# Relayout transfers that write every sixth row, into four tensors of their own

## The chip, the cores and the metric

The kernel runs on one core of a Trainium2 chip. The metric is device time in microseconds of one execution; lower is better. The kernel before took 726.89 us, the median of three runs (723.93 to 726.97).

## The reference

Three layers run one after the other, on 4 sequences of 768 positions.

```python
# 1. gated linear attention with a complex decay: 8 heads of 48
for t in range(S):
    ar, ai = (a_re_n[:, :, t, :, None], a_im_n[:, :, t, :, None])
    new_re = ar * S_re - ai * S_im
    new_im = ar * S_im + ai * S_re
    kv = np.einsum('bhd,bhe->bhde', k[:, :, t], v[:, :, t])
    S_re, S_im = (new_re + kv, new_im)
    y[:, :, t] = np.einsum('bhd,bhde->bhe', q[:, :, t], S_re)
# 2. feed-forward, 384 -> 1024 -> 384, gated by a convolution of 3 positions
h = np.maximum(x @ w_in, 0.0)
...
x = h * gate @ w_out
# 3. four experts of causal attention (width 64), the best two of each position summed
...
out += mask[..., None] * w[:, :, kk:kk + 1] * ye
```

## The kernel before

The recurrence is computed in chunks of C = 128 positions. A unit is UC = 2 chunks (256 positions); there are 12 units, three for each sequence. For each unit `e_ops` turns the decays into magnitudes and phases (`polar`, `phase`: running sums by matmuls with a triangle, L423, then exponentials and sines), and `rotate` multiplies q and k with them (`c.mul`, the helper at L380). The result of `rotate` lies with 384 rows (head dimension by head) as 3 tiles of 128 partitions. The chunk matmuls need it with 48 real and 48 imaginary rows on 96 partitions and the 8 heads beside each other. `put` does this relayout by DMA, from SBUF to SBUF: for kT and qT, real and imaginary half, one transfer for each of the 3 tiles, so 12 for a unit. A transfer reads 128 partitions and writes 16 rows of 8 heads. All are recorded by the helper at L386, and nearly all are issued on SP's queue; in the profile they are `arena_Z<-arena_F`.

For each chunk `m_ops` then multiplies scores out of kT and qT (L571, masked on VectorE at L573), transposes kT (L583, copied at L585), forms the state (L591, L600) and the output (L609 and L613, copied at L619), which goes to a scratch tensor in HBM. Stage two (`s2_ops`) loads it in half sequences and runs the feed-forward by nine matmuls a block up (L743) and nine down (L781). Stage three (`s3_ops`) projects (L851, L901), scores, takes softmaxes and sums.

No order is written out by hand. Each `S.op` names its engines with a cost in microseconds, the tiles it reads and writes, and a priority made of the numbers in the table `P` (`tu` is the pitch of units, `lag` the start of stage two in units, `u0`, `v0`, ... corrections for single units). `Sched.run` is a list scheduler on a model of the engines: it chooses for each op the time, the engine among those named, and the address, and `emit` writes the instructions in that order. On the chip each engine then runs its own list in order and waits on semaphores. Transfers are modelled as one pipe of 360 GB/s behind the issue, and land 0.9 us after it; a relayout counts 512 bytes for each column.

Tiles lie in arenas: F (float32), R (float32r, for stages two and three) and Z, which is used as float32 by stage one (Z0: kT, qT, v, masked scores, states) and as float32r (Z1) by the later stages once no op of stage one needs it (L148). While stage two's first loads are awaited, TensorE runs idle-filling matmuls on zeros (L627).

The lines of the relayout:

```python
r0 = 48 * half + 16 * i
c.load(lambda r0=r0: dst[r0:r0 + 16, :, x0:x1], lambda i=i: src[:, i, x0:x1], 512 * (x1 - x0), ...
```

Of the kernel before, what the change touches and what calls it, by code (L numbers as in the profile page):

```python
# [9 lines left out]
F32 = mybir.dt.float32  # L10
F32R = mybir.dt.float32r
# [27 lines left out]
P = dict(tu=24.81, lag=2.00, tf=3.56, dn=29.40, pa=28.16, pf=31.70, pp=31.74, ps=19.16, pr=12.98, kn=9.82, pd=-10.31,
         py=-3.49, cw=6.45, cs=6.91, ne=3, sw=16.78, slack=0.33, hold=1.18, wl=0.23, bl=0.07, bc=0.37, hy=7.13,  # L40
         tb=28.68, xp=-22.98, jq=-1.01, jp=3.08, jv=-4.00, ja=-2.33, jf=16.61, jt=5.79, ju=0.10, jw=0.26, na=13, no=3,
         nt=6, ns=4, nx=7, nq=14, th=0.46, fr=0.20, nc=3, sd=1, ck=-587.37, up=61.76, big=0, a0=1, a1=3, u0=-1.81,
         u1=0.00, u2=3.11, u3=0.02, u4=0.75, u5=-0.59, u6=-1.33, u7=0.35, u8=0.63, u9=-4.21, u10=-7.57, u11=2.39,
         v0=-0.17, v1=-0.88, v2=2.18, v3=0.27, v4=1.22, v5=1.18, v6=0.00, v7=-7.38, v8=-7.08, v9=-2.05, v10=0.00,
         v11=-2.62, b0=0.00, b1=-4.24, b2=-0.23, b3=-0.03, b4=-0.60, b5=-0.53, b6=-3.32, b7=-1.31, b8=-2.61, c0=0.92,
         c1=-2.99, c2=1.81, c3=-0.52, pw=0.34, sp=1.00, jg=-8.86, pm=-0.26)
TABS = {"E": "natural_log_exp_and_others", "T": "trig_and_small", "S": "sigmoid_and_others",
        "U": "silu_and_others", "X": "exp_and_others"}
CPY = ("ACT", "DVE", "POOL")
COLS = {"F": 19200, "R": 16420, "Z": 16200}  # L50


class Tl:
# [41 lines left out]
class Sched:  # L95
# [8 lines left out]
        self.newest, self.fifo = {}, False  # L104

    def tile(self, shape, dtype=F32, tag=None, bufs=0, regs=None, trim=0):
        t = Tl(self, shape, dtype, regs or (("R", "Z1") if dtype == F32R else ("F",)), tag, bufs, trim)
        self.tiles.append(t)
        return t

# [34 lines left out]

    def place(self, t, live, z0):
        for reg in t.regs:
            if reg == "Z1" and z0:  # L148
                continue
            k = reg[0]  # L150
            pos = 0
            for a, b, _ in live[k]:
                if a - pos >= t.size:
                    break
                pos = max(pos, b)
            if self.cap[k] - pos >= (t.size if k == "P" else max(t.size, t.n)):
                return reg, pos
        return None

    def run(self):  # L160
# [5 lines left out]
        live = {k: [] for k in self.cap}  # L166
        counts, frees, left, gops = {}, [], {}, {}
        dma, curtab, now, port, narrow = 0.0, None, 0.0, 0.0, 0.0
        z0 = sum(1 for t in self.tiles if t.left and "Z0" in t.regs)
        for o in self.ops:  # L170
            if o.nd == 0:
                for e in o.alts:
# [25 lines left out]
        while done < total:  # L198
# [11 lines left out]
            while frees and frees[0][0] <= now:  # L210
                _, _, t = heapq.heappop(frees)
                live[t.reg[0]].remove((t.off, t.off + t.size, t.tag))
                counts[t.tag] -= 1
                if "Z0" in t.regs:
                    z0 -= 1
            pick = None
            later = inf
# [172 lines left out]
def s1_ops(c):  # L390
# [10 lines left out]
    def e_ops(u):  # L401
# [6 lines left out]
        F, R = S.tile([128, KT, UT], tag="F", bufs=2, regs=zs), S.tile([128, KT, UT + 4], tag="R", bufs=2, regs=zs)  # L408
        w, n = S.tile([128, KT, UT], tag="w", bufs=2, regs=zs), S.tile([128, KT, UT], tag="n", bufs=2, regs=zs)
        q, k = S.tile([128, KT, UT], tag="q", bufs=1, regs=zs), S.tile([128, KT, UT + 4], tag="k", bufs=1, regs=zs)  # L410
        qT = S.tile([96, H, UT], tag="qT", bufs=2, regs=zr)
        kT = S.tile([96, H, UT + 4], tag="kT", bufs=2, regs=zr)
        v = S.tile([128, UC, H, 64], tag="v", bufs=2, regs=zr)
        parts = [(x, x + 1) for x in range(UC)] if u == 0 else [(0, UC)]
        t.update(qT=qT, kT=kT, v=v, last=(len(parts) - 1, None),
# [96 lines left out]
        def rotate(z, a, b):  # L512
# [11 lines left out]
            def put(dst, half, src, ext):  # L524
                x0, x1 = a * C, b * C + (UC if ext else 0)
                for i in range(KT):
                    r0 = 48 * half + 16 * i
                    c.load(lambda r0=r0: dst[r0:r0 + 16, :, x0:x1], lambda i=i: src[:, i, x0:x1], 512 * (x1 - x0),
                           [(dst, (z, r0))], pr + 2, r=ks(src) + ([(src, (9,))] if ext else []), dur=0.65,
                           gp=u < P["sd"])  # L530

# [501 lines left out]
def tile_kernel(ctx: ExitStack, tc: tile.TileContext, q, k, v, a_re, a_im,  # L1033
# [210 lines left out]
```

## Time and profile before

| what | value |
|---|---|
| median of three runs | 726.89 us |
| the profiled execution | 726.38 us |
| its span | 724.6 us |
| mean granted clock of TensorE | 0.952 of full speed |
| busy: TensorE, VectorE, ScalarE, GpSimd | 665.6, 563.1, 486.8, 86.7 us |
| SP's DMA queue | 75.04 MB, 44.3% of 16 DMA engines' span |

The span begins with the first instruction and ends with the last; some 1.8 us of the execution's time lie around it. Stage one and the part of stage two woven into it take the first 395 us, what is left of stage two some 65, and stage three the rest. An engine that is busy need not be the bound: it runs its list in order, and what ends the idle time before an instruction shows what it waited for. [...]

### The profile page before, as it was taken

The page shows a single profiled execution, that of the slowest core. Times are in us where ns is not written, and L with a number is a line of the kernel's source. Part 1 is how long each engine was busy: PE and PEld are TensorE (multiplying, and loading weights), DVE is VectorE, ACT ScalarE, POOL GpSimd, SP SyncE. Part 2 cuts the span into 40 slices and gives each one's busy share as a digit, 9 for nine tenths or more (in the row PEclk, how much of TensorE's full clock was granted, in tenths as well). Part 3 has the DMA queues.
Part 4 walks back from the last instruction along what each step waited for, and adds up shares of the span by engine and source line. Part 5 has one row for each costly group of instructions (what it writes and reads, how often), then busy time and mean ns, then how long its engine had stood idle before and what let it go on. Part 6 is the DMA issues. An engine that isn't in the chain of part 4 may idle for free.

```text
span 724.6 us, 13162 instructions
## 1 busy us (share of the span) xinstructions
PE 665.6 (92%) x4776; PEld 594.4 (82%) x4780; DVE 563.1 (78%) x1157; ACT 486.8 (67%) x1011; POOL 86.7 (12%) x139
## 2 busy tenths in 40 slices
PE   7789879889798898989999999999999999999995
PEld 4468668779798798889989999997787889888774
DVE  6975889799897897887864899978786666866761
ACT  7944984679578797697842676556756755865752
POOL 0621111021210111300100110001002100100101
PEclk9985997999999999999999999999999999999998
DMA  8967794955929938939383233020003000000002
GB/s 298 156 157 155 214 189 77 234 122 127 208 85 176 241 111 178 164 123 130 125 98 99 94 100 89 33 66 34 1 1 99 33 3 32 34 1 1 34 34 71
DMA packets 54603, 76.57 MB, mean 106 GB/s; under 512 B 5104, under 2 KB 45936, under 8 KB 54528
## 3 DMA queue, kind: packets, MB, share of 16 engines
q1 hardware_dynamic: 54240, 75.04, 44.3%
q0 software_dynamic: 288, 0.59, 0.5%
q8 instruction: 39, 0.64, 0.4%
q14 instruction: 36, 0.29, 0.2%
HBM read 42.51 MB, written 14.16 MB: 78 GB/s over the span
## 4 chain that ended last, share of the span: by engine, by line
PE 50%; DVE 9%; DMA 6%; ACT 3%; issue 1%; SPq 1%; POOL 0%; ACTq 0%; DVEq 0%; POOLq 0%
PE banks L781 8%; PE banks L743 6%; PE banks L958 5%; PE banks L901 5%; PE banks L1024 4%; DMA arena_Z<-arena_F 4%; PE banks L851 3%; PE banks L979 3%; PE banks L1000 3%; PE banks L1001 2%; PE banks L571 2%; PE banks L423 2%; DVE arena_F L380 1%; PE banks L591 1%; PE banks L609 1%
## 5 line engine op out<-in xcount | busy, mean ns | idle before, releaser
L743 PE MATMUL banks<-arena_R 128*128 128x384 f32 (+1 forms) x472 | 97.5, 348 | 2.1 <-ACT arena_F L754 1.0
L781 PE MATMUL banks<-arena_R 128*128 128x384 f32 (+1 forms) x486 | 99.0, 344 | 0.0
L370 ACT ACTIVATE arena_F<-banks 128x384 f32<-128x384 f32 (+4 forms) x156 | 65.7, 448 | 44.5 <-PE banks L1024 19.6
L743 PEld LDWEIGHTS banks<-arena_R 128*128 128x128 f32 x472 | 83.8, 192 | 5.7 <-ACT arena_F L754 1.7
L765 DVE SCALAR_TENSOR_TENSOR arena_F<-arena_F 128x384 f32<-128x384 f32 (+1 forms) x128 | 78.6, 633 | 11.0 <-ACT arena_F L762 9.9
L781 PEld LDWEIGHTS banks<-arena_R 128*128 128x128 f32 x486 | 84.9, 190 | 0.5 <-issue 0.5
L1011 ACT ACTIVATE arena_F<-banks,arena_F 128x128 f32<-128x128 f32 (+5 forms) x96 | 60.6, 640 | 17.2 <-DVE arena_F L1009 16.5
L370 ACT ACTIVATE arena_R<-arena_F 128x384 fp32r<-128x384 f32 (+2 forms) x76 | 40.2, 543 | 46.5 <-PE banks L781 18.9
L380 DVE TENSOR_TENSOR arena_F<-arena_F 128x768 f32<-128x768 f32 (+1 forms) x78 | 68.8, 906 | 2.5 <-ACT arena_F L437 1.9
L571 PE MATMUL banks<-arena_Z 96*128 96x128 f32 x384 | 57.7, 310 | 5.7 <-issue 3.5
L1009 DVE TENSOR_REDUCE arena_F<-banks 128x1 f32<-128x128 f32 (+5 forms) x96 | 56.8, 617 | 5.1 <-PE banks L1003 3.7
L571 PEld LDWEIGHTS banks<-arena_Z 96*128 96x128 f32 x384 | 54.0, 221 | 7.3 <-issue 7.3
L344 ACT ACT_TABLE_LOAD x45 | 57.7, 1283 | 1.5 <-PEq L1236 0.8
L380 DVE TENSOR_TENSOR arena_R<-arena_F,arena_R 128x384 fp32r<-128x384 f32 (+2 forms) x87 | 47.2, 558 | 11.9 <-PE banks L781 5.7
L1024 PE MATMUL banks<-ident,arena_F 128*128 128x128 f32 x336 | 48.6, 275 | 0.1
L573 DVE TENSOR_TENSOR arena_Z<-banks,tri 128x512 f32<-128x512 f32 x48 | 32.2, 684 | 21.0 <-PE banks L571 17.2
L583 PE MATMUL banks<-ident,arena_Z 96*128 96x96 f32 x160 | 23.1, 273 | 22.5 <-DMA arena_Z<-arena_F 16.7
L583 PEld LDWEIGHTS banks<-ident,arena_Z 96*128 96x128 f32 x160 | 18.3, 157 | 29.7 <-issue 10.8
L609 PE MATMUL banks<-arena_Z 128*64 128x128 f32 x384 | 39.7, 298 | 1.3 <-DVE arena_Z L600 1.3
L372 DVE COPY arena_F<-banks 128x384 f32<-128x384 f32 (+4 forms) x64 | 33.2, 530 | 9.5 <-PE banks L1024 6.1
L754 ACT ACTIVATE arena_F<-banks 128x384 f32<-128x384 f32 (+1 forms) x64 | 30.7, 485 | 14.4 <-PE banks L743 13.1
L958 PE MATMUL banks<-arena_F 128*64 128x384 f32 (+2 forms) x288 | 40.1, 420 | 0.0
(170 smaller groups left out, 1484.7 us busy)
## 6 DMA issues: line engine op xcount, KB each, us to landing
arena_Z<-arena_F SPq DMA_DIRECT2D x66, 129.0 KB, 4.4
arena_Z<-arena_F SPq DMA_DIRECT2D x66, 128.0 KB, 6.4
arena_F<-x_scr SPq DMA_DIRECT2D x12, 576.0 KB, 4.5
arena_Z<-v SPq DMA_DIRECT2D x12, 512.0 KB, 6.3
arena_F<-q SPq DMA_DIRECT2D x12, 384.0 KB, 5.8
arena_F<-k SPq DMA_DIRECT2D x12, 384.0 KB, 5.9
x_scr<-arena_Z SPq DMA_DIRECT2D x24, 192.0 KB, 4.5
out<-arena_F SPq DMA_DIRECT2D x24, 192.0 KB, 1.9
```

What stands on the lines that cost most here:

```text
L344: nc.scalar.preload_act_table_set(TABS[o.tab])
L370: self.A.activation(out(), in_(), AF.Copy)
L380: self.E[e].tensor_tensor(out(), a(), b(), op=self.OPS[op])
L571: PE.matmul(ps[:, i, :], kT[:, h, cs_], qT[:, h, cs_], start=True, stop=True)
L609: PE.matmul(ps[64 * i:64 * i + 64, g_, :], v[:, ci, 2 * g_ + i, :], sm[g_ // 2][:, 2 * (g_ % 2) + i, :], start=True, stop=(cc == 0))
L743: PE.matmul(ps.ap, wi[f][a][:, i * 128:(i + 1) * 128], x[i].ap, start=(n == 0), stop=(n == 8))
L765: S.op({"DVE": dve(no) + 0.06}, lambda e, i=i: V.scalar_tensor_tensor(cv.ap, h[:, i:i + no], cw[:, k3 + i:k3 + i + 1], cv.ap, op0=OP.mult, ...
L781: PE.matmul(o[:, i, :], a[:, m * 128:(m + 1) * 128], g_.ap, start=(f == 0 and n == 0 and len(g) == 1), stop=(f == FT - 1 and n == 2 and i ...
L958: PE.matmul(py[64 * r:64 * r + 64, :n], v[kb][:, o:o + HD], at[r][:, kb, :n], start=(kb == 0), stop=(kb == nk - 1))
L1009: S.op({"DVE": dve(n)}, lambda e: V.tensor_reduce(nm.ap, view(), axis=AX.XY, op=OP.min), r=[ps], w=[nm], prio=d)
L1011: S.op({"ACT": act(n) + 0.15}, lambda e: A.activation(a.ap.rearrange("p (x y) -> p x y", x=nb), view(), AF.Exp, bias=nm.ap, scale=-1.0, ac ...
L1024: PE.transpose(pt[:, z, :], a[:, (g_ + z) * 128:(g_ + z + 1) * 128], ident)
```

## The change

- A transfer now writes rows r0, r0 + 6, ... r0 + 90, with r0 = 3 x half + i, in place of 16 neighbouring rows. All six transfers of a tile fill the same 96 rows as before, in another order; kT and qT have the same order, so sums over these rows, and transposes multiplied back, give the same.
- kT and qT leave arena Z, which shrinks from 16200 to 8264 columns, for four tensors A, B, C and D of 2080 columns each (8 heads of 260). The later stages may use these too, as float32r, once stage one is through.
- The scheduler's model: a relayout counts 840 bytes for each column, not 512, and a transfer lands 1.1 us after its place in the pipe, not 0.9.
- Some 45 numbers of the table `P` are others, and with them the order on every engine. Of the table a line stands here.

```diff
-P = dict(tu=24.81, lag=2.00, tf=3.56, dn=29.40, pa=28.16, pf=31.70, pp=31.74, ps=19.16, pr=12.98, kn=9.82, pd=-10.31,
+P = dict(tu=22.99, lag=1.78, tf=3.56, dn=29.40, pa=28.16, pf=31.65, pp=31.74, ps=19.16, pr=13.53, kn=9.56, pd=-10.31,
...
-COLS = {"F": 19200, "R": 16420, "Z": 16200}
+COLS = {"F": 19200, "R": 16420, "Z": 8264, "A": 2080, "B": 2080, "C": 2080, "D": 2080}
...
-        t = Tl(self, shape, dtype, regs or (("R", "Z1") if dtype == F32R else ("F",)), tag, bufs, trim)
+        t = Tl(self, shape, dtype, regs or (("R", "Z1", "A1", "B1", "C1", "D1") if dtype == F32R else ("F",)), tag, bufs, trim)
...
-            if reg == "Z1" and z0:
+            if reg[-1] == "1" and z0:
...
-                o.end = dma + 0.9
+                o.end = dma + 1.1
...
-        qT = S.tile([96, H, UT], tag="qT", bufs=2, regs=zr)
-        kT = S.tile([96, H, UT + 4], tag="kT", bufs=2, regs=zr)
+        qT = S.tile([96, H, UT], tag="qT", bufs=2, regs=("A0", "B0", "C0", "D0"))
+        kT = S.tile([96, H, UT + 4], tag="kT", bufs=2, regs=("A0", "B0", "C0", "D0"))
...
-                    r0 = 48 * half + 16 * i
-                    c.load(lambda r0=r0: dst[r0:r0 + 16, :, x0:x1], lambda i=i: src[:, i, x0:x1], 512 * (x1 - x0),
+                    r0 = KT * half + i
+                    c.load(lambda r0=r0: dst[r0:96:2 * KT, :, x0:x1], lambda i=i: src[:, i, x0:x1], 840 * (x1 - x0),
                            [(dst, (z, r0))], pr + 2, r=ks(src) + ([(src, (9,))] if ext else []), dur=0.65,
```

The order moves on all engines. On SP, the queue that issues the relayouts, the set of unit 4 stood like this before (names: `arena_F` to `arena_Z` with 16x8x258 is kT, with 16x8x256 is qT; x_scr is the scratch tensor between stages one and two):

```order
L386 DMA arena_F<-x_scr 128x3x386
L386 DMA arena_F<-w_out 128x768
L386 DMA arena_Z_113<-arena_F 16x8x258 x3
L386 DMA arena_Z_113<-v 128x1024
L386 DMA x_scr<-arena_Z_113 48x4x256
L386 DMA arena_Z_113<-arena_F 16x8x258 x3
L386 DMA arena_Z_113<-arena_F 16x8x256 x6
L386 DMA x_scr<-arena_Z_113 48x4x256
L386 DMA arena_F<-q 128x768
L386 DMA arena_F<-k 128x3x256
```

and stands like this now (A is kT, B is qT):

```order
L386 DMA arena_F<-x_scr 128x3x386
L386 DMA arena_A_240<-arena_F 16x8x258 x6
L386 DMA arena_B_261<-arena_F 16x8x256
L386 DMA arena_F<-w_in 128x768
L386 DMA arena_B_261<-arena_F 16x8x256 x2
L386 DMA arena_F<-k 128x3x256
L386 DMA arena_F<-a_im 128x768
L386 DMA arena_B_261<-arena_F 16x8x256 x3
L386 DMA x_scr<-arena_Z_113 48x4x256 x2
L386 DMA arena_F<-q 128x768
```

The load of v and a store left the middle of the set; a load of w_in, and the loads of k and of the next decays, now stand between transfers of qT.

On TensorE, around the first transposes of kT (L583) of unit 6, before:

```order
L423 MATMUL banks<-trit,arena_F 128x128 x6
L743 MATMUL banks<-arena_R 128x384 x9
L781 MATMUL banks<-arena_R 128x386 x9
L583 MATMUL banks<-ident,arena_Z_113 128x96 x4
L423 MATMUL banks<-tri,arena_F 128x128 x6
L583 MATMUL banks<-ident,arena_Z_113 128x96 x4
L743 MATMUL banks<-arena_R 128x384 x9
L571 MATMUL banks<-arena_Z_113 128x128 x8
```

and now:

```order
L781 MATMUL banks<-arena_R 128x384 x9
L571 MATMUL banks<-arena_D_976,arena_C_436 128x128 x4
L423 MATMUL banks<-trit,arena_F 128x128 x3
L781 MATMUL banks<-arena_R 128x386 x9
L583 MATMUL banks<-ident,arena_A_240 128x96 x4
L781 MATMUL banks<-arena_R 128x386 x9
L423 MATMUL banks<-trit,arena_F 128x128 x3
L781 MATMUL banks<-arena_R 128x386 x9
L583 MATMUL banks<-ident,arena_A_240 128x96 x4
```

Blocks of nine down matmuls (L781) now stand ahead of each of these transposes and behind it, and the running sums (L423) are cut into pieces of three.

On TensorE, at the end of stage one (the last output matmuls L609 and L613), before:

```order
L609 MATMUL banks<-arena_Z_113 64x128 x2
L613 MATMUL banks<-arena_Z_113 48x128 x2
L743 MATMUL banks<-arena_R 128x386 x54
L781 MATMUL banks<-arena_Z_3376,arena_R 128x386 x9
L743 MATMUL banks<-arena_R 128x386 x9
```

and now:

```order
L609 MATMUL banks<-arena_Z_113 64x128 x2
L613 MATMUL banks<-arena_D_976,arena_Z_113 48x128 x2
L781 MATMUL banks<-arena_R 128x384 x9
L648 MATMUL banks<-ones,arena_F 1x1
L781 MATMUL banks<-arena_R 128x384 x27
L743 MATMUL banks<-arena_R 128x386 x2
```

More of stage two's down matmuls are left for the time behind stage one: of the 576 in all, 360 stood ahead of the last L613, and 315 do now. The number of up matmuls ahead of it, 360, is the same. Elsewhere, 13 of the 64 multiplies of 768 columns that VectorE had pass to GpSimd (51 are left), the activation tables are loaded 40 times and not 45, and the matmuls on zeros are 96 and not 98.

## Rows read from the trace of the kernel before

**Rows 1.** Page, part 1: each engine's busy us, share of the span, instructions.

```profile
PE 665.6 (92%) x4776; PEld 594.4 (82%) x4780; DVE 563.1 (78%) x1157; ACT 486.8 (67%) x1011; POOL 86.7 (12%) x139
```

**Rows 2.** Windows, twelve around relayouts: us, engines' busy us (count), clock, DMA share, GB/s.

```profile
24.00:36.00 12.00, 8.64 (x52) 5.48 (x50) 11.48 (x26) 10.60 (x20) 5.85 (x9) 0.87 1.13 156
48.00:61.00 13.00, 8.32 (x48) 5.35 (x44) 9.75 (x21) 3.95 (x8) 0.00 (x0) 0.75 1.05 135
90.00:105.00 15.00, 11.49 (x65) 9.81 (x65) 13.32 (x28) 14.20 (x25) 0.66 (x5) 1.00 1.01 152
121.00:134.00 13.00, 10.59 (x80) 9.34 (x78) 11.20 (x21) 5.07 (x10) 0.10 (x1) 0.87 1.11 152
153.00:168.00 15.00, 12.11 (x84) 11.05 (x79) 14.88 (x28) 12.57 (x24) 1.22 (x7) 1.00 0.96 177
183.00:196.00 13.00, 9.46 (x86) 8.54 (x84) 12.60 (x22) 6.08 (x11) 1.80 (x3) 1.00 1.11 179
218.00:232.00 14.00, 11.58 (x91) 11.10 (x91) 11.72 (x23) 11.51 (x26) 0.14 (x2) 0.88 1.09 151
240.00:253.00 13.00, 10.13 (x83) 9.42 (x83) 10.22 (x18) 8.48 (x14) 2.52 (x3) 0.87 1.07 187
271.00:283.00 12.00, 9.79 (x80) 9.31 (x80) 8.16 (x14) 6.52 (x13) 1.83 (x2) 0.86 0.95 162
295.00:309.00 14.00, 11.72 (x91) 11.22 (x89) 10.82 (x18) 7.85 (x12) 4.02 (x8) 1.00 1.13 168
329.00:343.00 14.00, 14.00 (x113) 13.53 (x112) 10.13 (x16) 10.34 (x19) 0.27 (x4) 1.00 1.09 137
362.00:375.00 13.00, 11.82 (x87) 11.36 (x87) 10.57 (x22) 7.78 (x17) 0.24 (x3) 1.00 1.08 121
sum 161.00, PE 129.64 PEld 115.52 DVE 134.87 ACT 104.94 POOL 18.65; mean PE 10.80 PEld 9.63 DVE 11.24 ACT 8.75 POOL 1.55
```

**Rows 3.** Windows, most of stage one as a single stretch.

```profile
24.00:395.00 371.00, 332.00 (x2601) 306.77 (x2603) 303.01 (x559) 260.77 (x468) 53.70 (x80) 0.92 0.71 150
```

**Rows 4.** Windows, two stretches of 2 us: relayouts alone, then loads.

```profile
56.00:58.00 2.00, 2.00 (x11) 1.32 (x10) 0.49 (x2) 0.90 (x2) 0.00 (x0) 0.50 1.13 119
138.00:140.00 2.00, 2.00 (x29) 1.95 (x29) 1.97 (x5) 1.99 (x4) 0.00 (x0) 1.00 1.03 415
```

**Rows 5.** Waits, TensorE then SP: us in total, times, longest us.

```profile
PE banks L583 <- DMA arena_Z<-arena_F: 16.7, 7, 4.5
...
SPq L386 <- DMA arena_Z<-arena_F: 16.0, 24, 2.8
```

**Rows 6.** DMA issues, the relayouts: count, KB each, median us to landing.

```profile
arena_Z<-arena_F SPq DMA_DIRECT2D x66, 129.0 KB, 4.4
arena_Z<-arena_F SPq DMA_DIRECT2D x66, 128.0 KB, 6.4
```

**Rows 7.** Instructions on arena_Z: ns min/median/max, first and last start us; landings.

```profile
L613 PE MATMUL banks<-arena_Z x320: 270/272/421, 46.7 to 394.2; 96*48 96x128 f32 x160
...
L386 SPq DMA_DIRECT2D arena_Z<-arena_F x147: 547/594/1877, 21.9 to 367.7; - x147
...
DMA to landing us min/median/max: 2.7/5.4/9.0
```

**Rows 8.** Timeline of SP, then TensorE, unit 6: start us, us, [idle before <-releaser].

```profile
217.10 8.97 SPq L386 DMA_DIRECT2D arena_Z<-arena_F  x12
...
227.07 0.52 PE L583 MATMUL banks<-ident,arena_Z 96*128 96x96 f32 x4 [2.42 <-DMA arena_Z<-arena_F]
```

**Rows 9.** Groups by line, the multiply helper: busy us, mean ns, idle before.

```profile
L380 DVE TENSOR_TENSOR arena_F<-arena_F 128x768 f32<-128x768 f32 (+1 forms) x78 | 68.8, 906 | 2.5 <-ACT arena_F L437 1.9 <-ACT arena_F L507 0.2
...
L380 POOL TENSOR_TENSOR arena_F<-arena_F 128x768 f32<-128x768 f32 x13 | 26.9, 2067 | 54.9 <-DVE arena_F L380 17.8 <-issue 15.7 <-ACT arena_F L754 10.1
```

**Rows 10.** Chain of waits, one block of nine down matmuls: start us, us.

```profile
358.11 1.58 PE banks L781 x9
```

More of the change, by code (lines that the diff above doesn't have):

```diff
@@ L38 @@
 TINY64 = 1.125 * 2.0 ** -15
-P = dict(tu=24.81, lag=2.00, tf=3.56, dn=29.40, pa=28.16, pf=31.70, pp=31.74, ps=19.16, pr=12.98, kn=9.82, pd=-10.31,
[L40 to L46, printed above, removed]
+P = dict(tu=22.99, lag=1.78, tf=3.56, dn=29.40, pa=28.16, pf=31.65, pp=31.74, ps=19.16, pr=13.53, kn=9.56, pd=-10.31,
+         py=-3.49, cw=7.07, cs=6.91, ne=3, sw=16.78, slack=0.33, hold=1.18, wl=0.23, bl=0.07, bc=0.37, hy=7.06,
+         tb=28.68, xp=-21.85, jq=-1.43, jp=3.08, jv=-4.00, ja=-2.43, jf=16.61, jt=5.79, ju=0.10, jw=0.26, na=13, no=2,
+         nt=6, ns=4, nx=7, nq=14, th=0.46, fr=0.20, nc=2, sd=1, ck=-587.37, up=61.76, big=0, a0=1, a1=4, u0=-0.59,
+         u1=0.11, u2=3.11, u3=-0.41, u4=0.75, u5=1.55, u6=-0.26, u7=1.62, u8=0.57, u9=-4.01, u10=-7.57, u11=-0.52,
+         v0=-0.57, v1=-0.88, v2=2.18, v3=0.15, v4=1.22, v5=1.18, v6=0.00, v7=-7.38, v8=-7.08, v9=-5.79, v10=3.04,
+         v11=-7.00, b0=0.00, b1=-4.24, b2=-0.23, b3=7.87, b4=-0.60, b5=-0.53, b6=-3.32, b7=-1.95, b8=-2.61, c0=0.89,
+         c1=-2.69, c2=1.81, c3=-0.52, pw=0.14, sp=1.00, jg=-4.92, pm=-1.39)
 TABS = {"E": "natural_log_exp_and_others", "T": "trig_and_small", "S": "sigmoid_and_others",
@@ L168, in run @@
         dma, curtab, now, port, narrow = 0.0, None, 0.0, 0.0, 0.0
-        z0 = sum(1 for t in self.tiles if t.left and "Z0" in t.regs)
+        z0 = sum(1 for t in self.tiles if t.left and any(x[-1] == "0" for x in t.regs))
         for o in self.ops:
@@ L213, in run @@
                 counts[t.tag] -= 1
-                if "Z0" in t.regs:
+                if any(x[-1] == "0" for x in t.regs):
                     z0 -= 1
@@ L1079, in mem @@
                     else:
-                        got[reg] = pa.tile([128, COLS[reg[0]]], F32R if reg in ("R", "Z1") else F32, tag=reg[0],
+                        got[reg] = pa.tile([128, COLS[reg[0]]], F32R if reg == "R" or reg[-1] == "1" else F32, tag=reg[0],
                                            name="arena_" + reg)
```

## The prediction

> **What bounds the kernel now.** I read the engine shares first: TensorE is busy for 92% of the span, VectorE for 78% [rows 1]. An average over three stages doesn't say where time can be had, so I went on to windows. Stage one, with stage two woven into it, ends near 394.5 us: the last L613 matmul of the chunks starts at 394.2 [rows 7]. Each of its 12 units issues one set of relayout transfers (twelve of some 128 KB; unit 0 in halves). I laid a window around each set. The 12 windows take 161 us, and in them TensorE is busy for 129.64, so idle for 31.4 us; VectorE is idle for 26.1 [rows 2]. In the whole stretch from 24 to 395 us TensorE is idle for 39.0 us [rows 3]. Four fifths of its idle time thus lie where relayouts run, in 43% of the stretch.
>
> The rates say why. While only relayouts run, the queues move 119 GB/s at a DMA share of 1.13; whole-row loads move 415 GB/s at a share of 1.03 [rows 4]. The DMA engines are as occupied while they move less than a third as much, so something behind them is slow. A set is 6 x 129 + 6 x 128 KB [rows 6], 1.58 MB: 13.3 us at 119 GB/s, though SP could issue it in 12 x 0.594 = 7.1 us [rows 7]. It took 8.97 us for the set at 217.10 [rows 8], since SP waits for earlier relayouts to land: 24 times, 16.0 us in all [rows 5]. The matmul that transposes kT (L583) waited 16.7 us, in seven waits, for these landings [rows 5]; the one at 227.07 is 2.42 us long [rows 8].
>
> A second cost follows from the idle time. [...] Over 24 to 395 us the clock's mean is 0.92 [rows 3]: 0.08 x 371 = 29.7 us of full speed not granted.
>
> **The change part by part.**
>
> *Rows of the relayout.* No transfer of before writes rows six apart, so I bound it. At worst the rate stays at 119 GB/s; a layout that is slower still I leave to the range. At best it reaches that of whole rows, 415 GB/s: then 1.58 MB takes 3.8 us, and SP's 7.1 us of issue is the bound. I take the issue bound, some 222 GB/s: what differs between the two rates is where rows land, and the change spreads them over 96 rows where before all 16 went to neighbouring ones. [...]
>
> With 0.594 us between issues and the quickest landing of before, 2.7 us [rows 7], kT's sixth transfer lands 5 x 0.594 + 2.7 = 5.7 us after the set's first issue; before it is 5 x 0.75 + 4.4 = 8.2 us (8.97 / 12 = 0.75, and the 4.4 us of [rows 6]). That is 2.5 us earlier. The twelfth lands at 9.2 instead of 11 x 0.75 + 6.4 = 14.6 us. So a set's idle time can shrink by 2.5 us where kT ends it. With each of the 12 idle times cut at 2.5 (six are longer; the others are 2.41, 2.42, 2.21, 2.28, 1.18 and 0) they sum to 25.5 us [rows 2]. Of the 16.7 us put down to landings the longest wait, 4.5, keeps 2.0: 14.7. Between 14.7 and 25.5 I take 18, nearer the waits themselves, since other idle time in the windows has other releasers. Late next is VectorE, busy for 134.9 of the 161 us.
>
> *The clock.* If half of the loss stays away with the idle times, 15 us of speed come back. Where TensorE is slow but VectorE is what it will wait for, that gives nothing, so I count half of it again: 7 us. The bounds are 0 and 29.7.
>
> *The order of TensorE.* In unit 6 a wait of 2.42 us stands behind a group of L423, nine L743 and nine L781, with nothing more to do [rows 8]; in the changed order a block of nine L781 stands ahead of each L583 there and behind it. That hides what is left of such a wait, and I count it in the 18. Five blocks of nine L781 pass from before the last chunk to behind it (360 L781 stood ahead of it, now 315): 5 x 1.58 us = 7.9 us [rows 10]. They cost nothing as long as stage one ends 7.9 us sooner; what stands behind it is TensorE's work either way.
>
> *VectorE to GpSimd.* 13 of VectorE's 64 multiplies of 768 columns change engine. VectorE loses 13 x 0.91 = 11.8 us; GpSimd takes 13 x 2.07 = 26.9 us [rows 9]. Each is up to 1.16 us later for what reads it, often a relayout on SP's queue, behind which loads are queued: between a gain of 11.8 us and a cost of 13 x 1.16 = 15.1. I take 4 us of cost, about a quarter of them on the path. [...]
>
> *The rest.* Five activation table loads fewer on ScalarE, whose busy time is far from the span's; heat matmuls 98 and now 96; a shifted order in stage three, whose work is the same. Zero.
>
> **The sum.** 18 + 7 - 4 = 21 us. The profiled execution took 726.38 us (its span is 724.6, the rest lies around it), half a microsecond below the median of the runs, 726.89: 726.4 - 21 = 705.4, so 705 us.
>
> **Rivals.**
> *It gives more.* If the order fits the landings so well that the whole 25.5 us goes, half of the clock's loss (15) shortens the end in full and GpSimd costs nothing, it is 40 us, so 686. For it: both engines have their idle time in the same windows. Against it: VectorE is busy for 303 of 371 us [rows 3] and would have 291 us of work in some 331.
>
> *VectorE's chain takes over.* Landings come sooner, but the multiplies ahead of them, late on GpSimd, set the pace: 18 us less half of the 15.1 is 10, with no clock gained: 716. It decides where SP waits longer than before for L380.
>
> *The waits only move.* Idle time leaves L583 and comes back ahead of L423 or L571: within 0.5% of before, 723 to 730, which is about what a measurement here can't tell from no change.
>
> *Slower.* The rate is not set by where rows land, and stays at 119 GB/s. Stage one then keeps its length, and the five L781 blocks put behind it come on top: 726.4 + 7.9 = 734. It decides at a stage one that ends less than 7.9 us earlier than 394.5. For it: SP needs its 0.594 us an issue whatever the rows, and engines at a share of 1.13 look full. Against it: the same engines moved 415 GB/s at 1.03.
>
> **How the numbers follow.** 705 (697 to 713): 0.48. More, 686: 0.17. VectorE's chain, 716: 0.15. No change: 0.06. Slower, 734: 0.14. The first three are faster by over 0.5%: 0.80; the others give 0.06 and 0.14. The range reaches from 688, with about half of the second case below it, to 730, which leaves out most of the slower one: some 2 in 10 in all.
>
> **What would show it.** Right: over 190 GB/s where only relayouts run, sets issued in under 8 us, median landings below 4 us in both of that table's relayout rows; less than 6 us of waits of L583 for landings; the last L613 near 365 (394 - 21 - 7.9); a mean clock above 0.95 in stage one. Wrong: the rate still near 119; or a good rate, and TensorE idle for over 35 us of stage one behind VectorE, GpSimd or loads on SP's queue; or the part behind stage one longer by more than the 7.9 us of L781.

## The result, and the profile after

The changed kernel takes 693.45 us (median of 4 runs, 691.31 to 697.06) against 726.93 (723.93 to 727.04) for the kernel before on the same chip: a ratio of 0.9554 [0.9507, 0.9601]. The forecast was 705, with a range of 688 to 730. The time lies inside that range, 3.5 us below the forecast's own one (697 to 713), and nearer to the rival "it gives more" than to the middle of the forecast. The profiled execution took 693.14 us with a span of 691.3; the rows of after are from it. Medians are of all executions of a version; the ratios leave out those over 1.5% above the fastest of the same kernel and are not quotients of the medians.

Part 1 of the page of after (busy us, share, instructions; DVE is VectorE, ACT ScalarE, POOL GpSimd, PE TensorE, PEld its weight loads), which answers to [rows 1]:

```profile
PE 648.2 (94%) x4774; PEld 577.4 (84%) x4778; DVE 564.1 (82%) x1144; ACT 478.7 (69%) x1003; POOL 113.7 (16%) x157
```

VectorE's busy time is the same as before (563.1), although 13 multiplies left it for GpSimd. What stayed on VectorE took longer: its 51 multiplies of 768 columns have a mean of 1058 ns, the 64 of before 979; `mul_dve` below shows more.

The last L613 matmul, which ended stage one's chunks at 394.2 us [rows 7], of after:

```profile
L613 PE MATMUL banks<-arena_D,arena_Z x128: 270/272/310, 128.9 to 351.4; 96*48 96x128 f32 x128
```

It starts 42.8 us earlier. The windows of after (us, busy us and count of PE, PEld, DVE, ACT, POOL, granted clock, DMA share, GB/s) split at this place:

```profile
0.00:351.60 351.60, 321.41 (x2624) 291.04 (x2628) 315.91 (x591) 273.85 (x499) 83.32 (x100) 0.97 0.59 176
351.60:691.30 339.70, 326.77 (x2153) 286.33 (x2151) 248.15 (x553) 204.87 (x504) 30.35 (x57) 0.99 0.14 44
```

and the same two of before:

```profile
0.00:394.40 394.40, 349.11 (x2671) 316.08 (x2675) 320.66 (x617) 280.30 (x501) 59.75 (x88) 0.92 0.72 157
394.40:724.60 330.20, 316.49 (x2108) 278.29 (x2106) 242.43 (x540) 206.48 (x510) 26.95 (x51) 0.99 0.14 45
```

Stage one: TensorE's idle time fell from 45.3 us (394.40 - 349.11) to 30.2, by 15.1, and its busy time from 349.11 to 321.41, by 27.7. Of these the five blocks of L781 that left it are 7.9 [rows 10]; the other 19.8 are matmuls that ran faster. The clock fits: the speed not granted fell from 31.6 us (0.08 x 394.4) to 10.5 (0.03 x 351.6), by 21, some of it in idle time. Behind it, TensorE has 45 matmuls more, the five blocks of nine, and the part is 9.5 us longer. The net of 33.3 is the span's (724.6 to 691.3).

Where the time came from is seen at the relayouts (transfers of kT and qT). Two windows of 2 us of after in which only relayouts run, to set beside the first of [rows 4]:

```profile
46.00:48.00 2.00, 0.09 (x1) 0.00 (x0) 2.00 (x5) 0.00 (x0) 0.00 (x0) 1.00 0.74 201
154.00:156.00 2.00, 2.00 (x13) 2.00 (x13) 2.00 (x3) 1.56 (x3) 2.00 (x7) 1.00 0.73 197
```

They move 201 and 197 GB/s at a DMA share of 0.74 and 0.73, where before it was 119 at 1.13. The issues of after (count, KB each, median us to landing) answer to [rows 6], whose medians were 4.4 and 6.4:

```profile
arena_C<-arena_F SPq DMA_DIRECT2D x36, 129.0 KB, 2.4
...
arena_B<-arena_F SPq DMA_DIRECT2D x36, 128.0 KB, 2.4
...
arena_A<-arena_F SPq DMA_DIRECT2D x30, 129.0 KB, 2.7
arena_D<-arena_F SPq DMA_DIRECT2D x30, 128.0 KB, 2.4
```

SP's timeline of after, the set that was issued quickest, with C for kT and D for qT:

```profile
259.75 3.78 SPq L386 DMA_DIRECT2D arena_C<-arena_F  x6
263.62 3.81 SPq L386 DMA_DIRECT2D arena_D<-arena_F  x6
```

This set is issued in 7.7 us: SP goes from one transfer to the next without waiting. It is not typical: the other ten whole sets (units 1 to 11) take 8.2 to 16.8 us, since other transfers stand between theirs, and the mean is 9.6, where it was 9.3 before (7.7 to 11.5). What became shorter is the landing: by the trace, kT's sixth transfer lands 6.9 us after a set's first issue, where it was 9.6, and the twelfth 11.8, where it was 15.5. Of the waits of [rows 5], this is left on TensorE (total us, times, longest), after the two longest of other kinds:

```profile
PE banks L423 <- ACT arena_F L467: 7.1, 3, 2.9
PE banks L423 <- DVE arena_F L449: 3.7, 3, 1.8
...
PE banks L583 <- DMA arena_C<-arena_F: 2.5, 1, 2.5
```

The 16.7 us behind landings became 2.5, and the first places are held by ScalarE and VectorE. The sum of the twelve windows around sets, which answers to [rows 2]:

```profile
sum 172.00, PE 151.39 PEld 138.85 DVE 163.95 ACT 125.13 POOL 39.19; mean PE 12.62 PEld 11.57 DVE 13.66 ACT 10.43 POOL 3.27
```

TensorE is idle for 20.6 of 172 us (31.4 of 161 before). VectorE is idle for only 8.1, where it was 26.1: it is the likely next limit.

### The profile page after: what moved, and what is told of

It reads as the page before. It is cut to its first block, busy times and chain, and to the rows that moved or that the text cites. A ratio compares the mean times of both kernels' runs of the same rounds, so it can differ in the third digit from the quotient of the medians.

```text
span 691.3 us, 13153 instructions
## 1 busy us (share of the span) xinstructions
PE 648.2 (94%) x4774; PEld 577.4 (84%) x4778; DVE 564.1 (82%) x1144; ACT 478.7 (69%) x1003; POOL 113.7 (16%) x157
## 4 chain that ended last, share of the span: by engine, by line
PE 63%; DVE 19%; ACT 8%; DMA 5%; issue 3%; SPq 1%; DVEq 0%; ACTq 0%
PE banks L781 12%; PE banks L743 10%; PE banks L958 6%; PE banks L901 5%; PE banks L1024 4%; PE banks L571 4%; PE banks L851 3%; PE banks L979 3%; DVE arena_F L380 3%; PE banks L1000 3%; PE banks L423 3%; DVE arena_R L380 3%; PE banks L1001 2%; PE banks L591 2%; PE banks L609 2%
## 5 line engine op out<-in xcount | busy, mean ns | idle before, releaser
L781 PE MATMUL banks<-arena_R 128*128 128x384 f32 (+1 forms) x510 | 104.1, 343 | 0.0
L743 PE MATMUL banks<-arena_R 128*128 128x384 f32 (+1 forms) x472 | 101.6, 343 | 2.4 <-DVE arena_Z L596 0.9
L781 PEld LDWEIGHTS banks<-arena_R 128*128 128x128 f32 x510 | 88.3, 188 | 1.7 <-issue 1.3
L370 ACT ACTIVATE arena_F<-banks 128x384 f32<-128x384 f32 (+4 forms) x145 | 61.9, 453 | 39.8 <-PE banks L1024 18.7
L765 DVE SCALAR_TENSOR_TENSOR arena_F<-arena_F 128x386 f32<-128x386 f32 (+1 forms) x128 | 77.5, 626 | 4.2 <-ACT arena_F L762 2.9
L380 DVE TENSOR_TENSOR arena_R<-arena_F,arena_R 128x384 fp32r<-128x384 f32 (+1 forms) x88 | 57.3, 668 | 14.6 <-PE banks L781 10.1
L380 POOL TENSOR_TENSOR arena_F<-arena_F 128x768 f32<-128x768 f32 x26 | 50.3, 1941 | 107.9 <-ACT arena_F L458 29.3
L380 DVE TENSOR_TENSOR arena_F<-arena_F 128x768 f32<-128x768 f32 (+1 forms) x65 | 61.0, 954 | 0.5 <-ACT arena_F L437 0.3
L754 ACT ACTIVATE arena_F<-banks 128x384 f32<-128x384 f32 (+1 forms) x64 | 31.0, 486 | 25.5 <-PE banks L743 21.7
L1000 PE MATMUL banks<-arena_R 128*128 128x384 f32 (+4 forms) x112 | 41.7, 375 | 1.6 <-ACT arena_F L1011 1.6
L372 DVE COPY arena_F<-banks 128x512 f32<-128x512 f32 (+4 forms) x75 | 37.6, 516 | 6.7 <-PE banks L1024 2.8
L609 PE MATMUL banks<-arena_Z 128*64 128x128 f32 x384 | 37.5, 283 | 3.9 <-DVE arena_Z L573 3.0
L1024 PEld LDWEIGHTS banks<-ident,arena_F 128*128 128x128 f32 x336 | 37.1, 141 | 3.2 <-ACT arena_F L370 1.3
L768 DVE SCALAR_TENSOR_TENSOR arena_F<-arena_F 128x384 f32<-128x384 f32 (+1 forms) x64 | 36.4, 588 | 3.6 <-ACT arena_F L767 3.2
L573 DVE TENSOR_TENSOR arena_Z<-banks,tri 128x512 f32<-128x512 f32 x48 | 31.9, 681 | 5.9 <-PE banks L571 5.2
```

The costliest lines, as they stand in the source:

```text
L370: self.A.activation(out(), in_(), AF.Copy)
L380: self.E[e].tensor_tensor(out(), a(), b(), op=self.OPS[op])
L609: PE.matmul(ps[64 * i:64 * i + 64, g_, :], v[:, ci, 2 * g_ + i, :], sm[g_ // 2][:, 2 * (g_ % 2) + i, :], start=True, stop=(cc == 0))
L743: PE.matmul(ps.ap, wi[f][a][:, i * 128:(i + 1) * 128], x[i].ap, start=(n == 0), stop=(n == 8))
L765: S.op({"DVE": dve(no) + 0.06}, lambda e, i=i: V.scalar_tensor_tensor(cv.ap, h[:, i:i + no], cw[:, k3 + i:k3 + i + 1], cv.ap, op0=OP.mult, ...
L781: PE.matmul(o[:, i, :], a[:, m * 128:(m + 1) * 128], g_.ap, start=(f == 0 and n == 0 and len(g) == 1), stop=(f == FT - 1 and n == 2 and i ...
```

## Experiments

All ratios are to the kernel before, executed beside each version on the same chip (medians of 727.66 to 728.85 us), with 95% intervals. Three parts can be taken apart: the tensors of their own, the rows, and the order with the engines of its multiplies.

### Own tensors and rows, in the old order

`own`: the kernel before, with the tensors A to D but 16 neighbouring rows. Stages two and three, whose tiles may lie there too, are placed and ordered a little otherwise.

```diff
...
-COLS = {"F": 19200, "R": 16420, "Z": 16200}
+COLS = {"F": 19200, "R": 16420, "Z": 8264, "A": 2080, "B": 2080, "C": 2080, "D": 2080}
...
-        kT = S.tile([96, H, UT + 4], tag="kT", bufs=2, regs=zr)
+        kT = S.tile([96, H, UT + 4], tag="kT", bufs=2, regs=("A0", "B0", "C0", "D0"))
```

> The kernel before with kT and qT in four tensors of their own, rows as before (16 neighbours), table and model as before: stage one's order is unchanged, only some of stage two and three is ordered otherwise, since their tiles lie elsewhere. If the tensors do nothing by themselves (my theory): 723 to 731 us, relayouts still near 120 GB/s. If the move out of the arena is itself a gain: below 720.

731.23 us, 1.0057 [1.0019, 1.0095]; the last L613 starts at 400.0. The tensors alone give nothing; if anything they cost 0.6%.

`own_rows`: the same, and the rows six apart. The instructions of `own` and `own_rows` stand in the same order on every engine; only the rows differ.

```diff
-                    r0 = 48 * half + 16 * i
-                    c.load(lambda r0=r0: dst[r0:r0 + 16, :, x0:x1], lambda i=i: src[:, i, x0:x1], 512 * (x1 - x0),
+                    r0 = KT * half + i
+                    c.load(lambda r0=r0: dst[r0:96:2 * KT, :, x0:x1], lambda i=i: src[:, i, x0:x1], 512 * (x1 - x0),
```

> The same with rows six apart and nothing else: the rows alone, in the order of before. Theory A (the rate of the relayouts is the cause): 200 GB/s or more while only relayouts run, TensorE waits less than 6 us for their landings in stage one, and the time falls to 700 to 710 us, most of the 33 us. Theory B (the new order is the cause, the rows only fit to it): 715 to 727. Theory C (both are needed): near 715, halfway.

695.33 us, 0.9529 [0.9485, 0.9573], as much as the whole change and below the 700 to 710 of Theory A. Its last L613, its one kind of wait of L583 for landings, and the windows over stage one of `own` and `own_rows`:

```profile
L613 PE MATMUL banks<-arena_D,arena_Z x112: 270/272/275, 181.5 to 358.8; 96*48 96x128 f32 x112
```

```profile
PE banks L583 <- DMA arena_A<-arena_F: 1.1, 2, 0.7
```

```profile
24.00:400.00 376.00, 332.92 (x2600) 307.74 (x2598) 302.74 (x559) 260.54 (x467) 53.69 (x80) 0.91 0.72 147
```

```profile
24.00:359.00 335.00, 312.92 (x2605) 286.80 (x2604) 301.23 (x560) 259.68 (x468) 56.03 (x81) 0.98 0.57 166
```

Stage one ends 41.2 us sooner than in `own`. With the same matmuls in it, TensorE's idle time fell from 43.1 us to 22.1 and its busy time from 332.9 to 312.9, at a clock of 0.98 instead of 0.91: half of the gain is less idle time, half is faster matmuls. (The two profiled executions lie 40.8 us apart, the medians 35.9.)

`rows_arena`: the rows alone, with kT and qT left in arena Z; the edit is the four lines above on the kernel before.

> The kernel before with rows six apart but kT and qT left in the arena. The instructions stand in the order of before on every engine. The waits differ: a transfer that writes rows 0 to 91 of the arena is taken to touch columns of other tiles too, so VectorE's masking (L573) and ScalarE's copies (L585, L619) wait for transfers that they do not need. Theory: these waits give back a good part, 703 to 722 us. Rival: transfers land so early now that the waits cost nothing, 692 to 699, and the tensors of their own are not needed.

772.1 us, 1.0614 [1.0560, 1.0669]: slower than any expectation. The transfers are as quick as in `own_rows` (medians of 2.4 to 2.6 us there); the waits for them are not (all engines, up to 445 us):

```profile
arena_Z<-arena_F SPq DMA_DIRECT2D x66, 129.0 KB, 2.4
arena_Z<-arena_F SPq DMA_DIRECT2D x66, 128.0 KB, 2.4
```

```profile
ACT arena_Z L585 <- DMA arena_Z<-arena_F: 36.2, 11, 9.2
...
DVE arena_Z L573 <- DMA arena_Z<-arena_F: 25.7, 9, 5.3
```

L585 and L573 write evictions from PSUM to other tiles of arena Z and read nothing that a relayout wrote directly, yet ScalarE waits for 36.2 us and VectorE for 25.7. With a stride over the rows, a write seems to be ordered against its neighbours in the tensor as well; that is an inference from these waits alone. This is why the tensors belong to the change: 77 us lie between `rows_arena` and `own_rows`.

### The order alone

`order_only`: the changed kernel with 16 neighbouring rows.

```diff
-                    r0 = KT * half + i
-                    c.load(lambda r0=r0: dst[r0:96:2 * KT, :, x0:x1], lambda i=i: src[:, i, x0:x1], 840 * (x1 - x0),
+                    r0 = 48 * half + 16 * i
+                    c.load(lambda r0=r0: dst[r0:r0 + 16, :, x0:x1], lambda i=i: src[:, i, x0:x1], 840 * (x1 - x0),
```

> The changed kernel with 16 neighbouring rows: table, model, tensors and so the whole order are those of the change, only the rows are those of before. Theory A: the rate falls back to about 120 GB/s, the waits for landings come back, and the time is 715 to 735 us. Theory B: 690 to 705, since the blocks of down matmuls between the transposes of kT hide the slow landings.

725.39 us, 0.9967 [0.9936, 0.9998]. The last L613 starts at 386.2, 8.0 earlier than before: that is the 7.9 us of L781, put behind. The waits are there again:

```profile
PE banks L583 <- DMA arena_A<-arena_F: 9.3, 4, 3.4
PE banks L583 <- DMA arena_C<-arena_F: 4.4, 1, 4.4
```

Beside the kernel before, the order by itself is worth at most some 5 us. Beside `own`, which has the same tensors and rows and was run on the same chip, it is worth 5.8 (731.23 - 725.39, and the intervals don't touch).

### Which rows

`step2` and `step3`: the changed kernel with rows two and three apart.

```diff
-                    r0 = KT * half + i
-                    c.load(lambda r0=r0: dst[r0:96:2 * KT, :, x0:x1], ...
+                    r0 = 32 * ((KT * half + i) // 2) + (KT * half + i) % 2      # step2
+                    c.load(lambda r0=r0: dst[r0:r0 + 31:2, :, x0:x1], ...
+                    r0 = 48 * half + i                                          # step3
+                    c.load(lambda r0=r0: dst[r0:r0 + 46:3, :, x0:x1], ...
```

> The changed kernel, its order and all else, with rows two apart: a transfer writes 16 rows of 32 neighbouring ones. [...] Theory S (the rate grows with the stretch of rows that a transfer covers, 16, 32 or 91): some 130 to 160 GB/s, 705 to 720 us.

> The changed kernel with rows three apart, 16 of 46. [...] Theory S: better than rows two apart, 150 to 180 GB/s.

691.26 us, 0.9482 [0.9433, 0.9530], and 691.3, 0.9504 [0.9456, 0.9552]: both like six apart within the intervals. Landings have medians of 2.6 to 2.7 us with two apart and of 3.3 to 4.0 with three, so a wider spread of the rows isn't what counts: two apart lands sooner than three. The later landings of three apart cost nothing that can be seen.

`bench`: no kernel, but 36 transfers in each of eight trials, one layout after another, first from SP alone, then from SP and ScalarE in turn. It computes nothing of the reference.

```python
rows = {1: lambda g: slice(16 * g, 16 * g + 16), 3: ..., 2: ..., 6: lambda g: slice(g, 96, 6)}
for step, two in ((1, 0), (3, 0), (2, 0), (6, 0), (1, 1), (3, 1), (2, 1), (6, 1)):
    ...
            eng = nc.scalar if two and n % 2 else nc.sync
            eng.dma_start(d[rows[step](g), :, :], src[:, g % 3, :])
```

> Nothing but transfers of 128 KB in the shape of the relayout: 36 in a row with rows 1, 3, 2 and 6 apart, issued on SP; then the same four with SP and ScalarE's queue issuing in turn. It computes nothing of the reference and writes zeros. [...] Theory S: 1, 2, 3 and 6 apart come out in this order of rising rate; with two queues rows six apart gain most.

A window in each trial, in that order (us, DVE, POOL, clock, DMA share, GB/s):

```profile
20.00:40.00 20.00, 0.45 (x3) 0.00 (x0) 1.00 1.15 123
52.00:66.00 14.00, 0.45 (x3) 0.00 (x0) 1.00 1.08 197
77.00:90.00 13.00, 0.45 (x3) 0.00 (x0) 1.00 0.73 202
101.00:114.00 13.00, 0.45 (x3) 0.00 (x0) 1.00 0.73 202
130.00:150.00 20.00, 0.45 (x3) 0.00 (x0) 1.00 1.15 121
166.00:179.00 13.00, 0.45 (x3) 0.00 (x0) 1.00 1.14 204
193.00:204.00 11.00, 0.45 (x3) 0.00 (x0) 1.00 1.13 223
215.00:225.00 10.00, 0.30 (x2) 0.00 (x0) 1.00 1.14 225
```

Neighbouring rows move 121 to 123 GB/s whether one queue issues or two: the issue is not their bound. Two and six apart give 202 from SP at a share of 0.73, and 223 to 225 from two queues at 1.13 and 1.14: from SP alone the issue is their bound, some 0.65 us for 131 KB (131 KB at 202 GB/s). In these trials a share of 1.15 at 121 to 123 GB/s thus marks transfers that are held up where they land, since only the written rows differ, and 0.73 an issuer that can't keep up. Three apart gets 197 from one queue and 204 from two, at shares of 1.08 and 1.14: a second queue brings little there, so the issue alone is not its bound. Theory S's order of rising rate, 1, 2, 3 and 6 apart, does not come out: from SP it is 123, 202, 197 and 202.

### kT or qT

`kt_rows` and `qt_rows`: `own_rows` with only one of the two spread; q's rows and k's then don't pair.

```diff
+                    r0, w0 = (KT * half + i, 2 * KT) if dst is kT else (48 * half + 16 * i, 1)
+                    c.load(lambda r0=r0, w0=w0: dst[r0:r0 + 15 * w0 + 1:w0, :, x0:x1], ...
```

> The kernel before with its tensors moved out of the arena (order of before), rows six apart for kT alone; qT keeps 16 neighbouring rows. The contraction then pairs wrong rows of kT and qT, so what follows computes other numbers at the same cost. Theory K (my prediction's: kT's landing, the sixth of a set, ends the idle time, and only it counts): nearly all of the 33 us, 695 to 703. Theory E (the end of the whole set counts, the twelfth landing): about half of it, 708 to 718, since half of the transfers got faster.

> The same the other way round: rows six apart for qT alone, kT slow (kT and qT again do not match in rows, at the same cost). Theory K: little, 720 to 730. Theory E: about half, 708 to 718, as for kT alone.

706.49 us, 0.9713 [0.9653, 0.9772], and 709.63, 0.9746 [0.9693, 0.9800]; the last L613 starts at 374.5 and 382.7. From `own` (731.23) kT's rows alone give 24.7 us, qT's alone 21.6, both 35.9. Each gives over half, near Theory E and far from Theory K. Their windows over stage one, to set beside that of `own`:

```profile
24.00:375.00 351.00, 320.34 (x2602) 294.77 (x2603) 302.96 (x559) 259.37 (x468) 54.00 (x80) 0.95 0.62 158
```

```profile
24.00:383.00 359.00, 319.54 (x2599) 295.32 (x2601) 303.05 (x560) 259.90 (x469) 55.80 (x80) 0.94 0.66 155
```

kT's rows take 12.4 us of idle time and 12.6 of busy time away. qT's take 3.6 of idle time and 13.4 of busy time (this execution, 716.41 us, is the longest of the six). In `qt_rows` kT's sixth transfer lands 9.8 us after a set's first issue, as late as in `own` (10.0), the twelfth at 13.4 instead of 15.9. The waits of L583 in `qt_rows`:

```profile
PE banks L583 <- DMA arena_C<-arena_F: 11.2, 3, 5.9
PE banks L583 <- DMA arena_A<-arena_F: 3.5, 2, 1.9
PE banks L583 <- DMA arena_D<-arena_F: 1.5, 1, 1.5
```

They sum to 16.2 us, as good as the 16.7 of [rows 5], and yet stage one ends 17.3 us sooner than in `own`. The end of the set counted too. In before, three waits of L571, which reads qT, end with it, though the table of waits puts only the first down to a landing:

```profile
105.92 3.75 PE L571 MATMUL banks<-arena_Z 96*128 96x128 f32 x16 [2.27 <-DMA arena_Z<-arena_F]
...
135.71 2.02 PE L571 MATMUL banks<-arena_Z 96*128 96x128 f32 x16 [1.53 <-issue]
...
197.00 3.08 PE L571 MATMUL banks<-arena_Z 96*128 96x128 f32 x16 [1.93 <-issue]
```

By the trace the twelfth transfers of these sets land at 105.78, 135.51 and 196.69, just ahead. Quicker transfers of qT also leave the queue sooner for what stands behind them; what of the 21.6 us is that, no run separates.

### The clock

`heat`: the kernel before, with 94 matmuls on zeros (78 of 384 columns, 16 of 512) put in front of seven of the waiting ones, so that TensorE doesn't idle there.

```diff
...
+                    if ci == 0 and g_ == 0:
+                        for _ in range({1: 25, 3: 12, 6: 13, 7: 16, 8: 12}.get(u, 0)):
+                            PE.matmul(ps.ap.rearrange("p a b -> p (a b)"), c.cs["zero"][:, :128], c.cs["zero"][:, :384],
+                                      start=True, stop=True)
```

> The kernel before with 94 matmuls on zeros put right ahead of seven matmuls that waited for landings (L583 of units 1, 3, 6, 7, 8: 25, 12, 13, 16, 12 of 384 columns; L571 of units 2 and 5: 9 and 7 of 512), sized to fill most of each wait; the relayouts stay as slow as before. Theory A2 (of the 33 us some 20 are speed of TensorE that the waits cost through its clock): the mean granted clock of stage one rises from 0.92 to 0.95 or more and the time falls to 712 to 721 us, with the waits still there. Rival (the clock is a symptom, what ends the stretches is VectorE or the transfers): 723 to 731.

731.15 us, 1.0018 [0.9978, 1.0058]: nothing. The profiled execution is the longest of the twelve (736.44 us, mean clock 0.958), so its unit 1 shows what can happen and not how much it is worth. TensorE's timeline of before (start us, us, [idle before <-releaser]):

```profile
55.67 0.87 PE L583 MATMUL banks<-ident,arena_Z 96*128 96x96 f32 x4 [4.52 <-DMA arena_Z<-arena_F]
...
59.33 2.68 PE L591 MATMUL banks<-arena_Z 128*96 128x48 f32 x16
61.85 3.76 PE L571 MATMUL banks<-arena_Z 96*128 96x128 f32 x16
```

and of `heat`, where the added lines make L591 of L583, L599 of L591 and L575 of L571:

```profile
51.97 4.23 PE L588 MATMUL banks<-zero 128*128 128x384 bf16 x25
56.90 0.53 PE L591 MATMUL banks<-ident,arena_Z 96*128 96x96 f32 x4 [0.70 <-DMA arena_Z<-arena_F]
...
59.52 1.48 PE L599 MATMUL banks<-arena_Z 128*96 128x48 f32 x16
63.08 3.75 PE L575 MATMUL banks<-arena_Z 96*128 96x128 f32 x16 [2.08 <-issue]
```

In unit 1 the clock was kept (1.00 from 56 to 58 us, where before has 0.50): L599 takes 1.48 us instead of 2.68. From the first transposes to the end of that line it is 4.1 us (56.90 to 61.00) instead of 6.3. But L575, which reads qT, starts 6.2 us after the first transposes in both kernels (63.08 - 56.90, 61.85 - 55.67). The trace has no releaser for the 2.08 us of idle time, but it has the landing: the set's twelfth transfer lands at 62.77 in `heat` and at 61.54 in before, 0.31 us ahead of this line in both. The speed regained was waited away, and before it was the low clock that filled the wait for qT.

Over whole executions, speed came back without time: the mean clock of `heat` is 0.958 to 0.986, against 0.949 to 0.966 in the 17 executions of before beside it, and its quickest, 724.30 us at 0.986, is no quicker than the quickest of before, 723.88 at 0.966. That doesn't make the clock worth nothing. Among `heat`'s twelve executions, all of one program, the time falls as the clock rises, from 736.44 us at 0.958 to 724.30 at 0.986. What the added matmuls cost elsewhere is not separated.

### The multiplies

`mul_dve`: the changed kernel, with the 26 multiplies of 768 columns that it runs on GpSimd put on VectorE, at the same places.

```diff
-            self.E[e].tensor_tensor(out(), a(), b(), op=self.OPS[op])
+            self.E["DVE" if n == 2 * DM else e].tensor_tensor(out(), a(), b(), op=self.OPS[op])
```

> The changed kernel with all multiplies of 768 columns that are ordered on GpSimd (26) run on VectorE at the same place of the order. My prediction's term (13 of them late on GpSimd cost 4 us): some 4 to 8 us faster, 685 to 690. Rival: VectorE is the second bound of stage one (316 of 352 us busy), 26 x 0.95 = 25 us more for it lengthen stage one: 700 to 715.

685.16 us, 0.9406 [0.9359, 0.9453], the best version of all. The multiplies by shape (busy us, mean ns | idle before) of after, and then of `mul_dve`:

```profile
L380 DVE TENSOR_TENSOR arena_F<-arena_F 128x768 f32<-128x768 f32 x51 | 53.4, 1058 | 0.3 <-ACT arena_F L437 0.3
L380 POOL TENSOR_TENSOR arena_F<-arena_F 128x768 f32<-128x768 f32 x26 | 50.3, 1941 | 107.9 <-ACT arena_F L458 29.3 <-issue 24.9 <-DMA x_scr<-arena_Z 17.2
L380 DVE TENSOR_TENSOR arena_R<-arena_F,arena_R 128x384 fp32r<-128x384 f32 x56 | 36.7, 668 | 10.5 <-PE banks L781 6.8 <-ACT arena_R L370 2.0 <-issue 1.3
```

```profile
L380 DVE TENSOR_TENSOR arena_F<-arena_F 128x768 f32<-128x768 f32 x77 | 72.6, 953 | 0.5 <-ACT arena_F L437 0.5
L380 DVE TENSOR_TENSOR arena_R<-arena_F,arena_R 128x384 fp32r<-128x384 f32 x56 | 30.8, 562 | 10.2 <-PE banks L781 6.8 <-ACT arena_R L370 2.1 <-issue 1.3
```

Beside 26 multiplies on GpSimd, the 51 of 768 columns left on VectorE take 105 ns longer each and the 56 of 384 columns 106: 5.4 + 5.9 = 11.3 us. Other instructions of VectorE were held as well, as its whole busy time shows; the first line of `mul_dve`'s page:

```profile
PE 644.2 (94%) x4778; PEld 574.2 (84%) x4778; DVE 565.7 (83%) x1170; ACT 478.0 (70%) x1003; POOL 68.5 (10%) x131
```

With 26 multiplies more, 24.8 us (26 x 0.953), VectorE is busy for 565.7 us, and for 564.1 without them: moving them to GpSimd freed VectorE of 1.6 us, and the other 23.2 came back as longer instructions. Those are few and much longer: the 88 multiplies that write arena_R, most of them of 384 columns, have a median of 551 ns and a longest of 2201 in after, 552 and 1035 in `mul_dve`. A place in after:

```profile
204.87 3.94 POOL L380 TENSOR_TENSOR arena_F<-arena_F 128x768 f32<-128x768 f32 x2
```

```profile
205.08 4.15 DVE L380 TENSOR_TENSOR arena_R<-arena_F,arena_R 128x384 fp32r<-128x384 f32 x2
```

Two multiplies of 384 columns take 4.15 us beside two on GpSimd, where two of `mul_dve`'s take 1.1 (2 x 0.562). VectorE's two end at 209.23, some 0.4 us behind GpSimd's two at 208.81: at this place they run beside these for nearly the whole time.

`own_rows_mul`: `own_rows` with the same edit, for the 13 multiplies on GpSimd in the old order.

> Rows six apart in the order of before, and the 13 multiplies of 768 columns that this order has on GpSimd run on VectorE at the same place. In the changed order moving 26 of them gave some 8 us, so 13 should give some 4: 687 to 693. If what counted there was that they came with the change's order (late, right ahead of transfers): no gain, 693 to 698.

694.94 us, 0.9567 [0.9515, 0.9618], not told apart from `own_rows` (0.9529). In the old order the 13 cost no time that can be seen, though there too VectorE's busy time is only 3.4 us less with them (561.2 and 564.6) and not 12.4 (13 x 0.952, their mean in `own_rows_mul`). Between `own_rows_mul` and `mul_dve` only the order and the scheduler's model differ, and here the new one is worth 9.8 us (694.94 - 685.16, on two chips). In the change that gain and what its 26 GpSimd multiplies cost (8.3 us, 693.45 - 685.16) nearly cancel.

## Why the prediction was right, and where its sum was off

*The rows: right.* 197 to 201 GB/s, medians of 2.4 to 2.7 us, 2.5 us of waits of L583, a clock of 0.97 in stage one: these tests for "right" came out. Sets issued in under 8 us did not: one of eleven is, as was one before. That a set's issue would go from 8.97 to 7.1 us took one set for all; the mean stayed (9.3 and 9.6), and the gain is in the landings. The last L613, put near 365, starts at 351.4, and that is where the sum was short. Where transfers follow each other, SP's issue, taken as an estimate, is the bound that `bench` shows: 202 GB/s at 0.73 of share, and 225 as soon as a second queue issues. The rate was some 10% under the 222 taken.

*The idle time: near in size, its mechanism short.* 18 were predicted, 15.1 came in the change and 21.0 by the rows alone (`own` to `own_rows`). "So a set's idle time can shrink by 2.5 us where kT ends it" has kT right: its sixth transfer lands 3.0 us sooner (10.0 and 7.0 us after the first issue). It leaves out that qT's twelfth, there 4.6 us sooner (15.9 and 11.3), ends waits too, which `qt_rows` shows with 21.6 us. The 14.7 us taken as the lower bound are 14.3: a second wait, of 2.87 us, keeps something as well.

*The clock: the term that was mis-sized.* 7 were predicted; matmuls that ran faster are 19.8 us in the change and 20.0 by the rows alone. The bounds, 0 to 29.7, held. Halving the loss twice is the step that was off: it had half of the low clock stay and half of the rest wait for VectorE, but of the 31.6 us of speed not granted 21 came back, and nearly all of it shortened stage one. `heat` shows how this goes with the idle time: in unit 1, with 0.70 us of idle time ahead of the first transposes instead of 4.52, the clock behind it is 1.00 instead of 0.50. There the low clock filled time in which TensorE would have waited for qT, so a clock regained alone gives nothing, and with early landings both go (from `own` to `own_rows` 43.1 us of idle time become 22.1 and a clock of 0.91 becomes 0.98). The two terms together were 25 and came out at 34.9 (15.1 + 19.8). How much the clock would give by itself, no run shows, and that its loss is a symptom of the waits is argued from few places.

*The order: half right.* The 7.9 us of L781 moved as worked out (8.0 in `order_only`, 45 matmuls in the windows). The part behind stage one became 9.5 us longer, which by the prediction's own test speaks against it; 1.6 us stay unexplained. That the order is worth nothing of its own holds for the change as a whole, where its GpSimd multiplies eat what it gives; with the old rows it gives 5.8 us, and with the multiplies back on VectorE 9.8. Why, no run shows.

*VectorE to GpSimd: the sign right, its mechanism not.* 4 us of cost stood for 13 multiplies that end later. `mul_dve` puts 8.3 on all 26, and the rows show what costs: with them on GpSimd VectorE's own multiplies take longer, a mean of 1058 ns instead of 953 for 768 columns and of 668 instead of 562 for 384. The mean of 0.906 us by which the prediction reckoned doesn't show such a cost: it mixes 64 multiplies of 768 columns with 14 of 384 [rows 9]. By form, the 64 have 979 ns in before, against 952 in `own_rows_mul`, where none of these multiplies is on GpSimd:

```profile
L380 DVE TENSOR_TENSOR arena_F<-arena_F 128x768 f32<-128x768 f32 x64 | 61.2, 979 | 2.3 <-ACT arena_F L437 1.9 <-ACT arena_F L507 0.2
```

That 13 on GpSimd cost little time was right (`own_rows_mul`); it doesn't carry over to 26.

*The rivals.* "Slower" rested on a rate that stays at 119 GB/s. `order_only` is that case, and it took 725.39 us, not 734: stage one did end 8.0 us earlier, by just the work moved. "The waits only move" falls with the 2.5 us. "VectorE's chain" is not what held the change at 716, but with 8.1 us of idle time in 172 it is the likely next one. "It gives more" was nearest in size, for another reason: GpSimd was not free, and idle time fell by 15.1 us, not 25.5; the clock gave 19.8, not 15.

*Open.* The scheduler's figures for a relayout (840 bytes a column, 1.1 us) were not tried apart from the table `P`.

## What to carry to other kernels

A DMA share of 1.13 at 119 GB/s, under a third of the 415 of whole rows, went, for these transfers, with rows that held them up where they landed; in such a case try spreading a transfer's rows over the partitions (every second was enough here: 202 GB/s instead of 123 in `bench`), and give the destination a tensor of its own before doing so (695.33 us with it, 772.1 without). When transfers of one set feed two consumers, price the last landing as well as the first (21.6 us in `qt_rows`), and look for a low clock that hides a wait (`heat`: 731.15 us, no gain). Work moved to GpSimd was paid for here by VectorE's other instructions (24.8 us moved, 1.6 freed): compare their mean durations shape by shape, not only the sums.

## What was not expected of the hardware

- Rows two apart are as good as six: 202 GB/s from one queue and 223 to 225 from two. Three apart are hardly worse from one queue, 197, get 204 from two, and are no slower in the kernel (691.3 us, with two apart 691.26).
- Quick landings say nothing by themselves: `rows_arena` has them (2.4 us) and takes the longest (772.1 us); ScalarE's L585 waits 36.2 us for them there and VectorE's L573 25.7.
- With 26 multiplies of 768 columns on GpSimd, VectorE's of 384 go from a mean of 562 ns to 668 and its own of 768 from 953 to 1058, few of them being much longer (of those that write arena_R the median stays at 551 ns and the longest is 2201); moving 24.8 us of work to GpSimd freed VectorE of 1.6 us.
